# Small runs in four column quarters: output columns instead of chunks

## The chip, the core and the metric

The kernel runs on one core of a Trainium2 chip. A core has TensorE (matrix products; its weight loads are a row of their own in the trace), VectorE (DVE), ScalarE (ACT), GpSimd (POOL) and SyncE (SP, which here only issues DMA transfers). The metric is the device time of one launch in microseconds (us).

## What is computed

Three stages follow each other: a windowed attention, a mixture of experts with one expert per token, and a dense two-layer net. The change lies in the second:

```python
# x: 2304 tokens x 512, eight experts, w1[e]: 512 x 1024, w2[e]: 1024 x 512
e_idx = argmax(x @ w_gate + modality_bias[modality_id])
for e in range(8):
    mask = e_idx == e
    h = maximum(x[mask] @ w1[e], 0)
    out[mask] = gate_w[mask] * (h @ w2[e])
```

All of it is float32.

## The kernel before

Tokens are sorted by expert, and the experts are worked off in **steps** of 256 tokens (a "wide" run). A step has two halves. `half_a` makes the hidden layer in eight blocks of 128 rows (`l1_wide`, `fb` = 0 to 7), `half_b` the output in four blocks (`l2_wide`, `d` = 0 to 3). Operands of the wide run are split into a high and a low part, so that each product is three matmuls (`three`, line 644). Of each block ScalarE writes the high part (line 654 or 663) and VectorE the low part (line 655). Between the blocks other work is woven in by hand: the split of the next expert's weights (`resplit`, line 203, only where the expert changes), the conversion of the dense stage's weights from 64 bits (`cv`, lines 960 to 972, most of VectorE's work here), and the **small run**.

A small run takes what an expert has left over, at most 32 tokens (`SB` = 32), with unsplit float32 weights (`raw`). Whether a step has one is known only on the chip, so each piece stands in a branch (`small`, line 668). Its pieces are spread over the step: `small_x` at block 0 of `half_a`, `small_1` at block 2, `small_h` at block 4, `small_2` at block 0 of `half_b`, `small_y` at 2, `small_out` at 3. In step 1 they come later. Steps 7 and 8 stand in a branch of their own (`either`) with a wide and a narrow arm.

A stationary operand of 32 tokens fills only 32 of TensorE's 128 columns, so the small matmuls are put in the four quarters of 32 columns, whose results land in partitions 0 to 31, 32 to 63 and so on. Before the change each quarter takes another **chunk** of the sum. In `small_1` the quarters hold the four chunks of the 512 inputs, and each streams all 512 columns of a half of w1: two halves, eight matmuls. What stands in the four bands of 32 partitions are four partial sums. ScalarE copies them to `hs`; `small_h` transposes 128 x 128 pieces (four per half, eight in all); and `sum_h` on VectorE adds the bands (two reductions) and clips at zero. `small_2` does the same with the eight chunks of the hidden layer, two per quarter, `small_y` transposes four pieces, and `sum_y` adds their bands. `sum_h` and `sum_y` stand outside the branch: they run in each of the steps 1 to 8, small run or not.

`self.b.A`, `X` and `B` are banks of the accumulator memory (PSUM): `A` and `B` are those of `l1_wide` and `l2_wide`, `X` those of the transposes. In the trace `raw`, `hs`, `ps_e`, `ps_s`, `ps_r` keep their names, `x32` is `x` and `h32` is `h`. The dense stage begins with line 1419, after fourteen filler matmuls (line 865).

Of the kernel before, what the change touches and what calls it, by code (L numbers as in the profile page):

```python
# [10 lines left out]
F32 = mybir.dt.float32  # L11
# [7 lines left out]
ALU = mybir.AluOpType  # L19
AX = mybir.AxisListType  # L20
# [4 lines left out]
HP = H // 2  # L25
# [25 lines left out]
SB = 32  # L51
# [91 lines left out]
class Banks:  # L143
# [12 lines left out]
    def rest(self, st):  # L156
        self.early.close()
        ps = st.enter_context(self.tc.tile_pool(name="ps_e", bufs=1, space=PSUM, reuse_waits="tile"))
        p = [ps.tile([128, 512], F32, name=f"ps_e{i}") for i in range(4)]
        self.A[2:] = p[0:2]  # L160
        self.B = p[2:]
# [44 lines left out]
class Route:  # L206
# [54 lines left out]
    def columns(self, a, b, hi, width, c0=0):  # L261
        V = self.tc.nc.vector
        bc = [128, b - a, width]
        tau = self.cs[:, C_TAU + c0:C_TAU + c0 + width]
        hv = self.hv[:, a:b, 0:width]
        V.tensor_tensor(hv, tau.unsqueeze(1).to_broadcast(bc), hi[:, a:b].unsqueeze(2).to_broadcast(bc), op=ALU.is_equal)
        V.tensor_tensor(hv, hv, self.cs[:, C_VAL + a:C_VAL + b].unsqueeze(2).to_broadcast(bc), op=ALU.mult)

# [17 lines left out]
    def pick(self):  # L286
        nc, oh, n, cum = self.tc.nc, self.oh, N0_T, self.cum
        V = nc.vector
        r = self.before(self.banks.s[1], 0, n)
        V.tensor_tensor(self.v[:, 0:n], r[:, 0:n, :], oh[:, 0:n, :], op=ALU.mult)  # L290
        V.tensor_copy(cum, r[:, n, :])
        yield
# [240 lines left out]
class Moe:  # L533
# [18 lines left out]
    def rest(self, st):  # L552
        one = st.enter_context(self.tc.tile_pool(name="m_two", bufs=1))
        self.hidden(one)
        self.hs = one.tile([128, 2, 512], F32, name="hs")
        self.x32 = one.tile([128, HP, SB], F32, name="x32")
        self.h32 = one.tile([128, 8, SB], F32, name="h32")
        self.xg3 = one.tile([SB, XW], F32, name="xg3")
        self.xg[1] = [one.tile([128, XW], F32, name=f"xgb{i}") for i in range(2)]
# [117 lines left out]

    def small_1(self, s):
        nc, raw = self.tc.nc, self.w.keep
        for h in range(2):  # L680
            for c in range(HP):
                nc.tensor.matmul(self.b.B[h][SB * c:SB * c + SB, :], self.x32[:, c, :], raw[2 * h + c // 2][:, c % 2, :],
                                 start=True, stop=True)
            nc.scalar.copy(self.hs[:, h, :], self.b.B[h])

    def bands(self, ps, n):
        return ps.rearrange("p (f j t) -> p f t j", f=n, t=SB)

    def small_h(self, s):
        nc = self.tc.nc  # L690
        for h in range(2):
            ps = self.b.X[h]
            for f in range(4):
                q = slice(f * 128, (f + 1) * 128)
                nc.tensor.transpose(ps[:, q], self.hs[:, h, q], self.ident)

    def sum_h(self):
        V = self.tc.nc.vector
        for h in range(2):
            V.tensor_reduce(self.h32[:, 4 * h:4 * h + 4, :], self.bands(self.b.X[h], 4), axis=AX.X, op=ALU.add)  # L700
        V.tensor_scalar(self.h32, self.h32, 0.0, None, op0=ALU.max)

    def small_2(self, s):
        nc, raw = self.tc.nc, self.w.keep
        for f in range(8):
            j = SB * (f % 4)
            nc.tensor.matmul(self.b.A[0][j:j + SB, :], self.h32[:, f, :], raw[4 + f // 2][:, f % 2, :],
                             start=(f < 4), stop=(f >= 4))
        nc.scalar.copy(self.hs[:, 0, :], self.b.A[0])

    def small_y(self, s):
        nc = self.tc.nc
        ps = self.b.A[1]
        for c in range(HP):
            q = slice(c * 128, (c + 1) * 128)
            nc.tensor.transpose(ps[:, q], self.hs[:, 0, q], self.ident)

    def sum_y(self):
        self.tc.nc.vector.tensor_reduce(self.x32, self.bands(self.b.A[1], HP), axis=AX.X, op=ALU.add)

    def small_out(self, s):
        self.tc.nc.scalar.copy(self.xy[:, :, bass.ds(self.regs[s]["so"], SB)], self.x32)

    def close_gap(self):
        tc, nc, xy = self.tc, self.tc.nc, self.xy
# [53 lines left out]
    def half_a(self, s, wide, work, rt=None):  # L779
        at = {7: self.small_x} if s == 1 else {0: self.small_x, 2: self.small_1, 4: self.small_h}  # L780
        for fb in range(8):
            if s == 1 and fb == 2:
                self.small_ids(rt, work)
            if s == 1 and fb == 6:
                self.scale(2)
            if s == 1 and fb == 6:
                self.load_regs("sm", R_SM, 1, 5, [ENG.PE, ENG.Activation])
                self.scale3(1)
            if s > 1 and fb in (1, 3, 5):
                self.resplit(s, fb + 1, fb + 3)  # L790
            if fb in at:
                self.small(s, at[fb])
                if at[fb] == self.small_h:
                    self.sum_h()
            if s == 1 and fb == 1:
                self.resplit(1, 4, 8)
            if wide:
                self.l1_wide(fb)
                if s > 1 or fb > 1:
                    next(work, None)  # L800
                    next(work, None)
            if s > 1 and fb == 3:
                self.load_w(s, 0, 4)
        if s == 1:
            self.small(s, self.small_1)
            self.load_w(s, 0, 4)
        for _ in work:
            pass

    def half_b(self, s, wide, work, rt=None):  # L810
        late = s == 1
        off = bass.ds(self.regs[s]["off"], 256)
        for d in range(HP):
            if late and d == 1:
                self.load_regs("sm", R_SM, 5, 10, [ENG.PE, ENG.Activation])
                self.small(s, self.small_h)
                self.sum_h()
                rt.positions()
            if d == (3 if late else 0):
                self.small(s, self.small_2)  # L820
                self.load_w(s, 4, 8)
            if wide and s != 8 and d == (2 if late else 0):
                self.tx(s + 1, 0)
                self.tx(s + 1, 1)
            if not late and d == 2:
                self.small(s, self.small_y)
                if s > 0:
                    self.sum_y()
            if not late and d == 3:
                self.small(s, self.small_out)  # L830
            if wide:
                self.l2_wide(d, off)
            if d < 3:
                for _ in range(6):
                    next(work, None)
            if d == 2:
                self.scale3(s + 1)
                self.resplit(s + 1, 0, 2)
        if late:
            self.small(s, self.small_y)  # L840
            self.sum_y()
            self.small(s, self.small_out)
        for _ in work:
            pass
# [783 lines left out]
```

## Time and profile before

| | us |
|---|---|
| median of three runs | 771.34 (769.26 to 773.08) |
| the profiled execution | 769.39 |
| its span, first to last instruction | 767.6 |
| TensorE busy | 739.3 (96%) |
| TensorE weight loads busy | 658.5 (86%) |
| VectorE busy | 491.3 (64%) |
| ScalarE busy | 387.4 (50%) |
| five small runs, start of `small_1` | 177.0, 206.7, 236.4, 266.1, 322.2 |

Busy time of TensorE overlaps with itself: a matmul's bar is longer than the distance to the next one's start, so here distances between starts are read, not bars. Times in a timeline count from the span's start; "x16" is the number of instructions in a merged row, and the second column is its length from the first start to the last end.

### The profile page before, as it was taken

Reading aid. Unit: us, or ns where it says so; the run is one execution under the profiler, and the core shown is the slowest. Engines: PE = TensorE matmul, PEld = TensorE weight load, DVE = VectorE, ACT = ScalarE, POOL = GpSimd, SP = SyncE. Lnnn points to the kernel's source line nnn. Section 1 sums busy time; section 2 is a strip of 40 time slices with the busy share of each in tenths; the row PEclk is TensorE's granted clock in tenths of the full one; section 3 lists DMA queues with packets and bytes.
Section 4 is the critical chain, followed back from the end, with each engine's and each line's share of the span. In section 5 each row is a group of like instructions: output and inputs, shape, how many; then the busy total and the mean of one; then the engine's idle time right before and its main releaser. Section 6 shows DMA issues by size and latency. Waiting matters only on the chain. (4 is left out here: it accounts for less than half of the span.)

```text
span 767.6 us, 15236 instructions
## 1 busy us (share of the span) xinstructions
PE 739.3 (96%) x5537; PEld 658.5 (86%) x5539; DVE 491.3 (64%) x1149; ACT 387.4 (50%) x1008; POOL 99.3 (13%) x99
## 2 busy tenths in 40 slices
PE   8999879999999999999799999999999999999996
PEld 4888669988998899889799889888889888988895
DVE  3678886773887878986487777864444464344341
ACT  4878753223323323442376666775445566454453
POOL 3325542230110100000000000011000003000003
PEclk9999999999999999999999999999999999999999
DMA  7789951269898967932257777488544556455512
GB/s 205 201 234 296 268 174 44 59 186 331 292 324 275 336 193 253 318 115 75 80 183 286 275 266 284 164 298 304 192 151 163 219 219 227 159 198 216 190 55 82
DMA packets 66189, 161.05 MB, mean 210 GB/s; under 512 B 8416, under 2 KB 25824, under 8 KB 60080
## 3 DMA queue, kind: packets, MB, share of 16 engines
q1 hardware_dynamic: 62592, 148.58, 57.0%
q0 software_dynamic: 3360, 11.01, 4.3%
q8 instruction: 49, 0.80, 0.4%
q14 instruction: 44, 0.36, 0.1%
q10 hardware_dynamic: 144, 0.29, 0.1%
HBM read 118.82 MB, written 41.04 MB: 208 GB/s over the span
## 5 line engine op out<-in xcount | busy, mean ns | idle before, releaser
L1439 DVE SCALAR_TENSOR_TENSOR t<-x,t 128x384 f32<-128x384 f32 x92 | 51.4, 558 | 80.0 <-ACT t L1432 79.8
L1462 PE MATMUL d_o<-d_ob,gh 128*128 128x512 f32 x288 | 89.6, 392 | 0.0
L1462 PE MATMUL d_o<-d_plain,gh 128*128 128x512 f32 x288 | 89.6, 392 | 0.0
L644 PE MATMUL ps_e<-hh,whi 128*128 128x256 f32 x288 | 82.9, 288 | 2.0 <-PEq L668 0.9
L644 PE MATMUL ps_e<-hl,whi 128*128 128x256 f32 x288 | 81.1, 282 | 0.0
L644 PE MATMUL ps_e<-hh,wlo 128*128 128x256 f32 x288 | 81.1, 281 | 0.0
L1431 ACT ACTIVATE t<-x 128x384 f32<-128x384 f32 x92 | 48.3, 525 | 52.5 <-DVE x L1452 52.5
L1447 DVE TENSOR_TENSOR gl<-t,gh 128x384 fp32r<-128x384 f32 x96 | 53.2, 554 | 17.8 <-ACT gh L1440 15.7
L1440 ACT CAST gh<-t 128x384 fp32r<-128x384 f32 x96 | 49.4, 514 | 29.6 <-DVE t L1439 29.3
L1452 DVE TENSOR_TENSOR x<-d_y,d_u 128x384 f32<-128x384 f32 x46 | 25.5, 554 | 53.1 <-ACT d_u L1543 53.1
L1462 PEld LDWEIGHTS d_o<-d_plain,gh 128*128 128x128 f32 x288 | 52.9, 188 | 6.1
L1462 PEld LDWEIGHTS d_o<-d_ob,gh 128*128 128x128 f32 x288 | 52.8, 188 | 5.7
L644 PEld LDWEIGHTS ps_e<-hh,whi 128*128 128x128 f32 x288 | 54.5, 189 | 3.1 <-issue 2.3
L1462 PE MATMUL d_o<-d_ob,gl 128*128 128x512 f32 x144 | 57.2, 397 | 0.0
L1462 PE MATMUL d_o<-d_plain,gl 128*128 128x512 f32 x144 | 57.1, 396 | 0.0
L1543 ACT COPY d_u<-d_x 128x384 f32<-128x384 f32 x46 | 22.0, 479 | 65.1 <-PE d_x L1419 65.1
L644 PEld LDWEIGHTS ps_e<-hh,wlo 128*128 128x128 f32 x288 | 54.5, 189 | 0.0
L644 PEld LDWEIGHTS ps_e<-hl,whi 128*128 128x128 f32 x288 | 54.4, 189 | 0.0
L663 ACT COPY xy<-ps_e 128x256 f32 (+1 forms) x36 | 13.4, 373 | 79.6 <-PE ps_e L644 65.1
L1432 ACT ACTIVATE t<-t 128x384 f32<-128x384 f32 x96 | 50.5, 526 | 3.0
L1471 POOL DMA_INDIRECT out<-o,pid x18 | 17.9, 995 | 248.4 <-ACT o L1470 246.6
L1200 ACT ACTIVATE p<-ps_s,nb 128x96 f32<-128x96 f32 x144 | 47.1, 341 | 2.7 <-issue 0.4
(441 smaller groups left out, 1922.8 us busy)
## 6 DMA issues: line engine op xcount, KB each, us to landing
raw<-in_w SPq DMA_DIRECT2D x48, 512.0 KB, 7.1
d_ab<-cache SPq DMA_DIRECT2D x15, 1024.0 KB, 6.2
d_ab<-cache SPq DMA_DIRECT2D x15, 768.0 KB, 4.3
r<-in_w_in SPq DMA_DIRECT2D x16, 512.0 KB, 5.8
r<-in_w_out SPq DMA_DIRECT2D x16, 512.0 KB, 5.4
wsc<-cva SPq DMA_DIRECT2D x32, 256.0 KB, 4.2
cache<-d_ab SPq DMA_DIRECT2D x8, 1024.0 KB, 5.0
d_ob<-cache SPq DMA_DIRECT2D x8, 1024.0 KB, 7.5
```

Of the source, the lines that this page charges most:

```text
L644: self.tc.nc.tensor.matmul(ps, a, b, start=(i == 0 and j == 0), stop=(i == n - 1 and j == 2))
L663: nc.scalar.copy(self.xy[:, d, off], ps)
L1200: nc.scalar.activation(p[:, j, :], s[:, j, :], ACTF.Exp, scale=scale, bias=nb[:, j:j + 1], accum_out=su[:, j:j + 1])
L1431: nc.scalar.activation(b.t, x, ACTF.Relu, scale=0.5, bias=0.5)
L1432: nc.scalar.activation(b.t, b.t, ACTF.Square)
L1439: nc.vector.scalar_tensor_tensor(b.t, x, 1.0, b.t, op0=ALU.max, op1=ALU.min)
L1440: nc.scalar.copy(b.h, b.t)
L1447: nc.vector.tensor_tensor(b.l, b.t, b.h.bitcast(F32), op=sub)
L1452: nc.vector.tensor_tensor(x, bank, other, op=add)
L1462: nc.tensor.matmul(po[i], a[:, q], o[:, x, f, :], start=(first and j == 0), stop=(last and j == 2))
L1471: nc.gpsimd.indirect_dma_start(out=outs[n][:, :], out_offset=bass.IndirectOffsetOnAxis(ap=pid[:, n:n + 1], axis=0), in_=t, in_offset=None)
L1543: nc.scalar.copy(part[("p1", "u2", "u3")[j // 2]], bank)
```

## The change

Each quarter now makes **its own output columns** over all chunks. In `small_1` quarter `j` streams columns 256 j to 256 j + 255 of the hidden layer (of w1's half `j // 2`) for chunk 0, 1, 2, 3 in turn and sums them in its band of one bank: 16 matmuls of 256 columns in place of 8 of 512. `hs` is then 128 x 256 instead of 128 x 1024, `small_h` needs two transposes instead of eight, and what comes out is already summed: `relu_h` clips it in one VectorE instruction. `small_2` gives each quarter 128 of the 512 output columns over all eight chunks: 32 matmuls of 128 columns in place of 8 of 512. `small_y` needs one transpose instead of four, `sum_y` falls away, and `small_out` copies from the bank.

```diff
     def small_1(self, s):
         nc, raw = self.tc.nc, self.w.keep
-        for h in range(2):
-            for c in range(HP):
-                nc.tensor.matmul(self.b.B[h][SB * c:SB * c + SB, :], self.x32[:, c, :], raw[2 * h + c // 2][:, c % 2, :],
-                                 start=True, stop=True)
-            nc.scalar.copy(self.hs[:, h, :], self.b.B[h])
+        ps = self.b.B[0][:, 0:256]
+        for c in range(HP):
+            for j in range(4):
+                q = slice(j % 2 * 256, j % 2 * 256 + 256)
+                nc.tensor.matmul(ps[SB * j:SB * j + SB, :], self.x32[:, c, :], raw[2 * (j // 2) + c // 2][:, c % 2, q],
+                                 start=(c == 0), stop=(c == HP - 1))
+        nc.scalar.copy(self.hs, ps)
...
     def small_h(self, s):
-        nc = self.tc.nc
-        for h in range(2):
-            ps = self.b.X[h]
-            for f in range(4):
-                q = slice(f * 128, (f + 1) * 128)
-                nc.tensor.transpose(ps[:, q], self.hs[:, h, q], self.ident)
-
-    def sum_h(self):
-        V = self.tc.nc.vector
-        for h in range(2):
-            V.tensor_reduce(self.h32[:, 4 * h:4 * h + 4, :], self.bands(self.b.X[h], 4), axis=AX.X, op=ALU.add)
-        V.tensor_scalar(self.h32, self.h32, 0.0, None, op0=ALU.max)
+        for k in range(2):
+            q = slice(k * 128, (k + 1) * 128)
+            self.tc.nc.tensor.transpose(self.b.X[0][:, q], self.hs[:, q], self.ident)
+
+    def relu_h(self):
+        self.tc.nc.vector.tensor_scalar(
+            self.h32.rearrange("p (j k) t -> p k j t", k=2),
+            self.b.X[0][:, 0:256].rearrange("p (k j t) -> p k j t", k=2, t=SB), 0.0, None, op0=ALU.max)
 
     def small_2(self, s):
         nc, raw = self.tc.nc, self.w.keep
+        ps = self.b.A[0][:, 0:128]
         for f in range(8):
-            j = SB * (f % 4)
-            nc.tensor.matmul(self.b.A[0][j:j + SB, :], self.h32[:, f, :], raw[4 + f // 2][:, f % 2, :],
-                             start=(f < 4), stop=(f >= 4))
-        nc.scalar.copy(self.hs[:, 0, :], self.b.A[0])
+            for j in range(4):
+                nc.tensor.matmul(ps[SB * j:SB * j + SB, :], self.h32[:, f, :], raw[4 + f // 2][:, f % 2, j * 128:(j + 1) * 128],
+                                 start=(f == 0), stop=(f == 7))
+        nc.scalar.copy(self.hs[:, 0:128], ps)
 
     def small_y(self, s):
-        nc = self.tc.nc
-        ps = self.b.A[1]
-        for c in range(HP):
-            q = slice(c * 128, (c + 1) * 128)
-            nc.tensor.transpose(ps[:, q], self.hs[:, 0, q], self.ident)
-
-    def sum_y(self):
-        self.tc.nc.vector.tensor_reduce(self.x32, self.bands(self.b.A[1], HP), axis=AX.X, op=ALU.add)
+        self.tc.nc.tensor.transpose(self.b.A[1][:, 0:128], self.hs[:, 0:128], self.ident)
 
     def small_out(self, s):
-        self.tc.nc.scalar.copy(self.xy[:, :, bass.ds(self.regs[s]["so"], SB)], self.x32)
+        self.tc.nc.scalar.copy(self.xy[:, :, bass.ds(self.regs[s]["so"], SB)],
+                               self.b.A[1][:, 0:HP * SB].rearrange("p (c t) -> p c t", c=HP))
```

At the places that called `sum_h` stands `relu_h`; the calls of `sum_y` are gone.

TensorE around `small_2` of step 2 (the difference; `xgb` is the gathered input of the next step, whose eight transposes follow): one row of eight 512-column matmuls gives way to one of 32 with 128 columns, at the same place.

```order
 L668 COMPARE_AND_BRANCH
-L707 MATMUL ps_s_81<-raw,h_2059 32x512 x8
-L668 UNCONDITIONAL_BRANCH x2
-L775 UNCONDITIONAL_BRANCH
+L703 MATMUL ps_s_81<-raw,h_2059 32x128 x32
+L668 UNCONDITIONAL_BRANCH x2
+L765 UNCONDITIONAL_BRANCH
 L635 MATMUL ps_r<-cs,xgb_2061 128x128 x4
 L635 MATMUL ps_s_83<-cs,xgb_2062 128x128 x4
```

The quarters follow each other within a chunk, so that neighbours in this row lie in different quarters, as before.

VectorE in step 3, around `sum_h` before the change (`cva` and `r` are the conversion, `hl` is a low part of the hidden layer):

```order
L655 SCALAR_TENSOR_TENSOR hl_118<-ps_e_2038,hh_117 128x256
L964 TENSOR_SCALAR r_3202<-r_3202 128x512
L700 TENSOR_REDUCE h_2059<-ps_r 128x128
L775 UNCONDITIONAL_BRANCH
L700 TENSOR_REDUCE h_2059<-ps_s_83 128x128
L701 TENSOR_SCALAR h_2059<-h_2059 128x256
L655 SCALAR_TENSOR_TENSOR hl_2056<-ps_s_81,hh_2055 128x256
```

and the same place after it:

```order
L655 SCALAR_TENSOR_TENSOR hl_118<-ps_e_2038,hh_117 128x256
L951 TENSOR_SCALAR r_3240<-r_3240 128x512
L694 TENSOR_SCALAR h_2059<-ps_r 128x2x4x32
L765 UNCONDITIONAL_BRANCH
L655 SCALAR_TENSOR_TENSOR hl_2056<-ps_s_81,hh_2055 128x256
```

Three instructions have become one; their neighbours stand as they did.

## Rows read from the trace of the kernel before

**Rows 1.** Busy time by stretch: stretch, length, PE, PEld, DVE, ACT, POOL, clock, DMA.

```profile
173.00:293.00 120.00, 119.78 (x1014) 106.46 (x1015) 88.03 (x189) 36.92 (x86) 10.29 (x11) 1.00 0.86 291
293.00:374.00 81.00, 78.26 (x637) 73.41 (x636) 61.87 (x121) 29.35 (x59) 4.89 (x5) 1.00 0.51 170
374.00:381.40 7.40, 3.66 (x18) 2.74 (x17) 3.58 (x8) 3.12 (x8) 0.00 (x0) 1.00 0.20 63
```

**Rows 2.** One line's instructions, `small_1` (ns min/median/max; first and last start).

```profile
L682 PE MATMUL ps_e<-raw,x x80: 592/592/618, 177.0 to 323.5; 128*32 128x512 f32 x80
```

**Rows 3.** Timeline of TensorE and its weight loads in the first small run.

```profile
177.03 0.16 PEld L682 LDWEIGHTS ps_e<-raw,x 128*32 128x32 f32 x8
177.03 1.92 PE L682 MATMUL ps_e<-raw,x 128*32 128x512 f32 x16
177.49 0.13 PEld L682 LDWEIGHTS ps_e<-raw,x 128*32 128x32 f32 x4 [0.30 <-issue]
177.91 0.13 PEld L682 LDWEIGHTS ps_e<-raw,x 128*32 128x32 f32 x4 [0.30 <-issue]
178.88 0.39 PE L644 MATMUL ps_e<-xh,whi 128*128 128x256 f32 x1
...
181.85 0.60 PE L695 MATMUL ps_r<-cs,hs 128*128 128x128 f32 x4
182.29 0.60 PE L695 MATMUL ps_s<-cs,hs 128*128 128x128 f32 x4
182.65 0.36 PE L644 MATMUL ps_s<-xh,whi 128*128 128x256 f32 x1
...
188.35 0.28 PE L644 MATMUL ps_e<-xl,whi 128*128 128x256 f32 x1
188.56 1.92 PE L707 MATMUL ps_s<-raw,h 128*32 128x512 f32 x16
```

**Rows 4.** Attention's matmuls in two column halves: weight loads (timeline, then the line).

```profile
43.29 0.66 PEld L1232 LDWEIGHTS ps_o<-pt,v 96*64 96x64 f32 x20
...
L1232 PEld LDWEIGHTS ps_o<-pt,v x576: 132/138/231, 20.5 to 119.9; 96*64 96x64 f32 x192
```

**Rows 5.** Groups by line: VectorE's sums (busy us, mean ns, idle time before them).

```profile
L719 DVE TENSOR_REDUCE x<-ps_s 128x128 f32<-128x512 f32 x8 | 5.5, 685 | 1.6 <-PEq L668 1.6
L700 DVE TENSOR_REDUCE h<-ps_r 128x128 f32<-128x512 f32 x8 | 5.5, 685 | 1.8 <-PEq L668 1.8
L701 DVE TENSOR_SCALAR h<-h 128x256 f32<-128x256 f32 x8 | 2.4, 294 | 0.3
```

**Rows 6.** Timeline before `small_2` of step 7: VectorE, ScalarE, then TensorE.

```profile
329.73 0.68 DVE L700 TENSOR_REDUCE h<-ps_r 128x128 f32<-128x512 f32 x1
...
331.59 2.35 DVE L203 TENSOR_TENSOR wlo<-raw,whi 128x1024 fp32r<-128x1024 f32 x2
333.86 0.42 DVE L655 SCALAR_TENSOR_TENSOR hl<-ps_s,hh 128x256 fp32r<-128x256 f32 x1
...
329.79 1.98 ACT L201 CAST whi<-raw 128x1024 fp32r<-128x1024 f32 x2
...
333.51 0.28 PE L644 MATMUL ps_e<-xl,whi 128*128 128x256 f32 x1
334.38 2.04 PE L707 MATMUL ps_s<-raw,h 128*32 128x512 f32 x16 [0.59 <-PE ps_e L644]
```

**Rows 7.** Timeline from the last expert step to the dense stage.

```profile
374.45 0.68 DVE L719 TENSOR_REDUCE x<-ps_s 128x128 f32<-128x512 f32 x1
...
374.30 3.37 PE L865 MATMUL ps_r<-whi 128*128 128x512 f32 x14
381.44 0.58 PE L1419 MATMUL d_x<-d_B110h,d_plain 128*128 128x384 f32 x2 [3.77 <-DMA d_wo<-wsc]
```

**Rows 8.** Timeline of TensorE where step 8 jumps over a small run's piece.

```profile
362.00 0.28 PE L644 MATMUL ps_e<-xl,whi 128*128 128x256 f32 x1
362.43 0.35 PE L644 MATMUL ps_e<-hh,whi 128*128 128x256 f32 x1
```

More of the change, by code (lines that the diff above doesn't have):

```diff
@@ L554, in rest @@
         self.hidden(one)
-        self.hs = one.tile([128, 2, 512], F32, name="hs")
+        self.hs = one.tile([128, 256], F32, name="hs")
         self.x32 = one.tile([128, HP, SB], F32, name="x32")
@@ L679, in small_1 @@
         nc, raw = self.tc.nc, self.w.keep
-        for h in range(2):
-            for c in range(HP):
-                nc.tensor.matmul(self.b.B[h][SB * c:SB * c + SB, :], self.x32[:, c, :], raw[2 * h + c // 2][:, c % 2, :],
-                                 start=True, stop=True)
-            nc.scalar.copy(self.hs[:, h, :], self.b.B[h])
-    def bands(self, ps, n):
-        return ps.rearrange("p (f j t) -> p f t j", f=n, t=SB)
-    def small_h(self, s):
-        nc = self.tc.nc
-        for h in range(2):
-            ps = self.b.X[h]
-            for f in range(4):
-                q = slice(f * 128, (f + 1) * 128)
-                nc.tensor.transpose(ps[:, q], self.hs[:, h, q], self.ident)
@@ L793, in half_a @@
                 if at[fb] == self.small_h:
-                    self.sum_h()
+                    self.relu_h()
             if s == 1 and fb == 1:
@@ L816, in half_b @@
                 self.small(s, self.small_h)
-                self.sum_h()
+                self.relu_h()
                 rt.positions()
@@ L826, in half_b @@
                 self.small(s, self.small_y)
-                if s > 0:
-                    self.sum_y()
             if not late and d == 3:
@@ L840, in half_b @@
             self.small(s, self.small_y)
-            self.sum_y()
             self.small(s, self.small_out)
```

## The prediction

> **What bounds the kernel now.** I read the busy time by stretch first, since the share over the whole span mixes three stages. From 173 to 293 us, where four of the five small runs stand, TensorE is busy 119.78 of 120 us, VectorE 88 and ScalarE 37 [rows 1]. To 374 us, with the fifth small run and two narrower steps, it is 78.26 of 81. Only the passage to the dense stage has a hole (3.66 of 7.40). So in the expert stage TensorE sets the pace, and what is taken from or added to its stream moves the stage's end one for one. What VectorE or ScalarE saves is worth nothing unless a TensorE wait on it shows.
>
> Next, the first small run in the timeline. The bars can't be summed: a `small_1` pass shows 592 ns [rows 2], yet sixteen fit into 1.92 us [rows 3]. I read starts instead. The eighty passes are five runs of sixteen, and a run has eight matmuls, so each float32 matmul is two passes. The later weight loads come in fours at 177.49 and 177.91, 0.42 us apart, and (1.92 − 0.59) / 3 = 0.44 gives the same: four passes, one for each column quarter, go on together, and a **round** of four takes 0.43 us for 512 columns. Quarters do overlap before the change; it must keep that.
>
> **Term 1, transposes.** Eight become two and four become one: nine fewer per run. Four take 182.29 − 181.85 = 0.44 us from start to start [rows 3], so one takes 0.11. TensorE stands behind them without a gap. 9 × 0.109 = 0.98 us less per run.
>
> **Term 2, matmul passes.** The work in columns stays, the pieces get smaller. `small_1`: 16 matmuls of two passes are 32 passes, or 8 rounds of 256 columns, in place of 4 rounds of 512. `small_2`: 64 passes, or 16 rounds of 128, in place of 4 of 512. No row has such rounds of quarters. The rows on both sides are the 512-column rounds (0.43 us) and attention's matmuls in two halves, 64 columns wide, which are ten rounds in 0.66 us: (0.66 − 0.14) / 9 = 0.058 us each [rows 4]. A line through both gives 0.111 us for 128 columns and 0.217 for 256. `small_2`: 16 × 0.111 = 1.78 for 4 × 0.43 = 1.72, +0.06. `small_1`: 8 × 0.217 = 1.74, +0.02. I take +0.08 per run. Bounds: 0, if time goes by columns alone; and a floor for each pass, since a half's pass took 0.058 / 2 = 0.029 us whatever set that. Four such are 0.116, so `small_2` takes 16 × 0.116 = 1.86 (+0.14) and a run +0.16. Below nothing I see no reason: no column is left out.
>
> Terms 1 and 2 are −0.90 per run (−0.98 to −0.82), for five runs **−4.5 us** (−4.9 to −4.1).
>
> **Term 3, VectorE and ScalarE.** Per step VectorE loses two sums of 685 ns and a clip of 294, which become one clip that reads the accumulator bank; and `sum_y`, 685 [rows 5]. The new clip lies between 0.29, the clip now, and 0.42, a low part of equally many columns that reads a bank too [rows 6]. So some 2 us leave each step, and ScalarE's copies into `hs` shrink from three of 512 columns to one of 256 and one of 128. Through 293 us TensorE never waits for either, and this buys nothing. One place differs: step 7. There `small_2` starts 334.38 − 333.51 = 0.87 us after the last `l1_wide` matmul [rows 6], against 188.56 − 188.35 = 0.21 in the first run [rows 3]: 0.66 us idle. The row names its own engine, but what had just ended is VectorE's low part (333.86 + 0.42 = 334.28). That was queued behind the weight split, and this behind the sums. The order of these neighbours is unchanged. Sums and clip there cost 0.68 + 0.68 + 0.29 = 1.65 us, the new clip at most 0.42, so VectorE comes 1.2 us earlier; but the split also needs ScalarE's high part, which ends at 329.79 + 1.98 = 331.77, just after the split's start, so the first of the two pieces may not move and only the second can. I take −0.55, between 0 (ScalarE holds it all) and −0.66 (all idle time goes; then the last matmul is itself what comes last).
>
> **Term 4, the way to the dense stage.** Line 1419 starts 3.77 us after the fillers, put down to a DMA of `d_wo` [rows 7]. The fillers follow TensorE's last step, and the transfer is issued behind VectorE's last work, which follows TensorE too. So I let the whole passage slide with the stage: 0. `sum_y` at 374.45 disappears; if the passage hangs on it, up to another 0.6 us goes.
>
> **Other things that move.** The first two `raw` tiles are read until the end of `small_1` in either order, so their refill comes no earlier than now; DMA is 0.86 busy there [rows 1], but TensorE waits for none. `small_out` now reads the bank and not `x32`: one semaphore of TensorE instead of one of VectorE, later than `small_y` by a whole block, and behind it on ScalarE stands only the next high part. All this I cost at nothing; the cover is that ScalarE is busy 37 of 120 us.
>
> **Sum.** −4.5 − 0.55 = −5.05 us, between −4.1 and −6.2 (−4.9 − 0.66 − 0.6). The profiled execution took 769.39 us (span 767.6 and 1.8 around it), so it would take 764.3. It lies 1.95 below the median of the runs shown, 771.34; from the median the time is **766.3 us**. The bounds give 765.1 to 767.2.
>
> **Rivals.**
>
> *Weight loads come into the open: slower.* There are twice the loads in `small_1` and four times in `small_2`, 24 rounds in place of 8. A quarter's weights have 0.11 us of cover in `small_2` where they had 0.43. If a round's loads had to wait until the round before is done, each round would be longer by about 0.11 us, the distance between a load of four and the next at the rate of four in 0.13 [rows 3]: 24 × 0.11 = 2.64 per run, less 0.98, +1.66, five times +8.3, or 779.6 us. It decides from 0.98 / 24 = 0.04 us per round. Against it: the halves load in 132 to 138 ns and yet follow each other at 58 ns a pair [rows 4], and the eight loads at 177.03 stand within 0.16 us while the first passes run [rows 3]. For it: no row has quarters with so few columns. 0.05. [...]
>
> *The longer branch bodies cost a fetch: slower.* The body of `small_2` becomes four times as long (64 passes with their loads for 16), and steps without a small run jump over it. A jump over the short body takes 362.43 − 362.00 = 0.43 us from matmul to matmul [rows 8]. If the longer jump leaves what the engine has fetched, the nearest price is the idle time at the end of the stage, where TensorE also branches away: 3.77 [rows 7], 3.34 more. Skips in steps 1, 6 and 8 and the arms not taken in 7 and 8 make five places: 5 × 3.34 − 5.05 = +11.7, or 783.0 us. It decides from 5.05 / 5 = 1.0 us a place. Against it: three of the five steps with such places lie between 293 and 374 us, where TensorE idles 2.74 us in all [rows 1], so that no jump costs nearly that today. 0.04. [...]
>
> *The dense stage does not move: no change.* If line 1419's start hangs on transfers with their own schedule, TensorE ends 5 us earlier and waits 5 us longer: 771.3 us. For it: the row blames a DMA [rows 7], and the DMA share is 0.51 in the stretch before it. Against: the transfer is issued only after VectorE's last work, and the share is 0.20 there [rows 1]. 0.08.
>
> **How the numbers follow.** Forecast 0.83, the three rivals 0.05, 0.04 and 0.08. About 0.5%, 3.9 us, is what a measurement of this kernel can tell from no change: the three runs span 3.8. The forecast's −4.1 to −6.2 lies just beyond, and the scatter of the medians puts some 0.12 of its 0.83 within: faster 0.71, same 0.12 + 0.08 = 0.20, slower 0.09. For the range I take the bounds, 765.1 and 767.2, and add the distance between profile and median (2.0) on both sides, then widen above to 770 for a forecast that reaches the dense stage only in part: 763 to 770.
>
> **What would show it.** In the profile after: 32 passes of 256 columns and 64 of 128 columns per run, five runs; from `small_1`'s start to the next `l1_wide` matmul still about 1.85 us, `small_2` 1.7 to 1.9; a line of ten transposes and one of five; steps of about 28.8 us where two small runs stood 29.7 apart; `relu_h` at 0.29 to 0.42 us; `small_2` of step 7 some 0.2 us behind line 644; line 1419 near 376.4. The prediction falls if the weight loads of `small_2` have gaps of passes between them (first rival), if line 644 waits behind a skipped body for longer than now (second), or if line 1419 stays at 381 (third).

## The result, and the profile after

The changed kernel takes 761.92 us (median of four runs, 760.82 to 762.92), the kernel before, beside it, 771.51 (769.26 to 773.08). The ratio is 0.988, 95% interval 0.9861 to 0.9898: 9.6 us faster, where 5.05 were forecast and 763 was the range's lower end. The profiled execution took 762.92 us (span 761.1), so this profile lies 1.0 above its median, and the one of before 2.1 below its own. The two profiles therefore differ by 6.47 only.

Both executions can be laid on each other matmul by matmul, since nothing but the small runs' lines differs. Read from starts:

| stretch | before | after | difference |
|---|---|---|---|
| to the first `small_1` (attention, routing, steps 0 and 1) | 177.03 | 178.81 | +1.78 |
| from there to the last `l1_wide`/`l2_wide` matmul (line 644) | 197.14 | 191.82 | −5.32 |
| from there to the first dense matmul (line 1419, now 1406) | 7.26 | 4.98 | −2.28 |
| from there to the start of the last matmul | 379.32 | 378.59 | −0.73 |
| behind it and around the span | 8.63 | 8.72 | +0.09 |

The first row is not the change's: no changed matmul has run by then, and in the profiles of the experiments below, which leave that part alone too, the first `small_1` starts anywhere from 177.0 to 181.0 us. The rest makes −8.2. What lacks to 9.6 lies within the scatter of either kernel's four runs. Of 18 later executions of the kernel before, the ten with a mean granted clock of 0.987 or less took 770.5 to 773.2 us and the four with 0.993 to 0.995 took 767.8 to 769.6, and its profiled one, at 0.993, is of the second sort.

The forecast was made for the second row. Its rows in the changed kernel, first run (timeline: start, length, then line and shape; PE is TensorE):

```profile
178.81 1.93 PE L684 MATMUL ps_e<-raw,x 128*32 128x256 f32 x32
180.67 0.39 PE L644 MATMUL ps_e<-xh,whi 128*128 128x256 f32 x1
...
183.53 0.28 PE L644 MATMUL ps_e<-xl,whi 128*128 128x256 f32 x1
183.65 0.38 PE L691 MATMUL ps_r<-cs,hs 128*128 128x128 f32 x2
183.79 0.36 PE L644 MATMUL ps_s<-xh,whi 128*128 128x256 f32 x1
...
189.72 1.95 PE L703 MATMUL ps_s<-raw,h 128*32 128x128 f32 x64
191.60 0.66 PE L635 MATMUL ps_r<-cs,xgb 128*128 128x128 f32 x4
...
198.24 0.27 PE L708 MATMUL ps_s<-cs,hs 128*128 128x128 f32 x1
198.27 0.36 PE L644 MATMUL ps_e<-hh,whi 128*128 128x256 f32 x1
```

Against [rows 3]: `small_1` holds TensorE for 180.67 − 178.81 = 1.86 us (178.88 − 177.03 = 1.85 before), `small_2` for 1.88. The transposes of `small_h` take 183.79 − 183.65 = 0.14, where 182.65 − 181.85 = 0.80 stood; `small_y`'s one takes 0.03. Per run that is −0.98 by transposes and +0.04 by passes.

The third row of the table is the one that the forecast put at nothing. Timeline after, from the last matmul of the stage:

```profile
370.75 3.37 PE L852 MATMUL ps_r<-whi 128*128 128x512 f32 x14
375.62 0.58 PE L1406 MATMUL d_x<-d_B110h,d_plain 128*128 128x384 f32 x2 [1.49 <-DVE d_B110h L1387]
376.24 0.44 PE L1406 MATMUL d_x<-d_B110l,d_plain 128*128 128x384 f32 x1
```

The idle time ahead of the dense stage is 1.49 us, and ends with VectorE's cast of the operand; in [rows 7] it was 3.77 and put down to a DMA. VectorE was not late there: before the change the same cast ended at 378.85 + 0.36 = 379.21, 2.2 us ahead of the matmul.

```profile
378.85 0.36 DVE L1400 CAST d_B110h<-xy 128x384 fp32r<-128x384 f32 x1 [3.71 <-DVEq L139]
```

What TensorE did in that idle time stands in the instructions of line 139, where the jump over all steps from 9 on ends (count, then shortest/median/longest ns, then first and last start; PEldq is TensorE's sequencer). Before, then after:

```profile
L139 PEldq EVENT_SEMAPHORE  x2: 51/51/51, 377.7 to 380.7; - x2
...
L139 PEldq COMPARE_BRANCH  x1: 3668/3668/3668, 373.9 to 373.9; - x1
```

```profile
L139 PEldq EVENT_SEMAPHORE  x2: 51/51/51, 374.2 to 374.3; - x2
...
L139 PEldq COMPARE_BRANCH  x1: 3674/3674/3674, 370.4 to 370.4; - x1
```

The jump takes 3.67 us in both, while the fillers still run. Behind it stand two semaphore instructions of 51 ns each, neither of which waits. After the change they follow each other by 0.15 us; before, 3.03 us lay between them, in which TensorE executed nothing. A transfer of 16 KB of instructions started at 378.36 and ended at 379.50 in that time, which suggests that the engine was out of code; the experiments test it. This pause held the dense stage.

Behind it the clock was lower, too. Windows of the first dense matmuls (stretch, length, busy times, then the granted clock, DMA share, GB/s), before and then after:

```profile
381.44:384.80 3.36, 3.36 (x12) 3.36 (x13) 2.66 (x6) 0.20 (x1) 0.00 (x0) 0.60 0.94 253
```

```profile
375.62:378.50 2.88, 2.84 (x15) 2.53 (x16) 2.88 (x7) 2.88 (x8) 0.00 (x0) 1.00 0.66 156
```

After 3.77 us idle the granted clock was 0.60 in this window: 0.50 from 382.20 to 385.50 us, where the matmuls of 384 columns start 0.32 us apart, and, behind the window, 1.00 from 385.60 to 389.00, where they start 0.17 us apart. After 1.49 us idle it was 1.00. Over the first 4 us of the dense stage this brings 1.2 us more, of which 0.5 is given back some 20 us later, where a matmul of the changed kernel waits for `d_T40l` of VectorE: hence −0.73 in the table's fourth row. This price is not the pause's alone: in two experiments below (the first half alone, and 64 columns) the dense part was 1.0 us longer than the changed kernel's without a pause, after 1.64 and 1.59 us idle. With the first half alone the granted clock here was 0.68; with 64 columns that of the whole execution was 0.987, against 0.992 in the changed kernel's.

### The profile page after: what moved, and what is told of

Same layout as the page of the kernel before. It is cut to its first block, busy times and chain, and to the rows that moved or that the text cites. A ratio compares the mean times of both kernels' runs of the same rounds, so it can differ in the third digit from the quotient of the medians.

```text
span 761.1 us, 15743 instructions
## 1 busy us (share of the span) xinstructions
PE 735.3 (97%) x5814; PEld 662.6 (87%) x5814; DVE 477.2 (63%) x1125; ACT 381.7 (50%) x1003; POOL 99.2 (13%) x99
## 4 chain that ended last, share of the span: by engine, by line
PE 31%; issue 15%; DMA 1%; DVE 1%; POOL 1%; ACT 1%; POOLq 0%; SPq 0%; ACTq 0%
PE d_o L1449 16%; PE d_x L1406 8%; PE d_y L1406 6%; POOL out L1458 1%; DMA cache<-d_ob 1%; DMA d_wo<-wsc 1%; DVE d_rT L1381 0%; DVE d_ob L1075 0%; DVE gl L1434 0%; POOLq L1611 0%; SPq L1012 0%; ACT d_ob L1073 0%; ACT o L1457 0%; DVE x L1439 0%; ACT t L1418 0%
```

## The experiments

**Is it the place of TensorE's code?** To the kernel before, matmuls are added that are never executed, in a step that is jumped over:

```diff
+        if s == 10:
+            for _ in range(40):
+                tc.nc.tensor.matmul(self.b.X[0], self.w.hi[0][:, 0, 0:128], self.w.hi[0][:, 1, :], start=True, stop=True)
```

> The kernel before, with 40 filler matmuls (80 instructions of TensorE) put into step 10, which is jumped over with all steps from 9 on, so that nothing more is executed and only TensorE's code behind them stands at other places. Theory (where TensorE's jump to the dense stage lands in its code sets a second wait): the pause between the two semaphore instructions of line 139 at 377.7 and 380.7 us goes, line 1419 starts 2.3 us earlier after the last line 644 (7.2 us becomes about 4.9), its first thirty matmuls no longer take 0.32 us but 0.17, and the time falls by about 3.7 us, to some 767.8. Rival (the change's own work brought the passage forward, by the sum taken off VectorE or by the DMA of d_wo): nothing moves, 771.5.

Measured: 766.35 us against 771.03, ratio 0.9955 (0.9936 to 0.9975). The stage is as long as ever (197.16 us), the passage is 4.93 in place of 7.26, and the rest of TensorE's stream 378.09 in place of 379.32.

```profile
374.83 3.37 PE L865 MATMUL ps_r<-whi 128*128 128x512 f32 x14
379.64 0.58 PE L1422 MATMUL d_x<-d_B110h,d_plain 128*128 128x384 f32 x2 [1.45 <-DVE d_B110h L1403]
```

With `sum_y` and everything else of the old kernel in place, code that nobody runs makes it faster: by 4.7 us between the medians, by 3.5 (1.9 to 4.9) from the ratio. VectorE's chain and the DMA are as they were, and so are out as causes.

**Can the pause be brought back?** The same lines in the changed kernel, first 85 of them. These are 170 instructions, which by a rough count of the author's put the jump's target near where it was before the change. The count took it that places in the code repeat every 256 instructions, an assumption which no run had shown.

> The changed kernel with 85 fillers in step 10, also never executed. [...] Theory of the landing place: the second pause comes back, line 1406 starts about 2 to 3 us later after the last line 644 (4.99 becomes 7 to 8), the first dense matmuls are slow again, and the time rises by 3 to 4 us, to about 765.5. Rival (the shorter VectorE chain): nothing moves, 761.9.

Measured: 762.29 us, passage 4.92: the pause of 3 us did not come, and the time is the changed kernel's. The rough count was off. Counted in the compiled programs, TensorE's code behind the jump is moved by 2023 instructions against the kernel before, 25 short of a multiple of 256. If the pause belongs to a place that comes once in 256 instructions, as assumed, TensorE should stop not after one instruction but after 26. Behind the jump come seven semaphore instructions, ten weight loads and nine matmuls, 26 in all, and then the tenth matmul is late: it starts 0.42 us behind the ninth, in the changed kernel 0.17 (rows here, then there). Its operand had been ready since 376.41.

```profile
377.09 0.33 PE L1409 MATMUL d_x<-d_B210l,d_plain 128*128 128x384 f32 x1
377.51 0.51 PE L1409 MATMUL d_x<-d_B211h,d_plain 128*128 128x384 f32 x2
```

```profile
377.40 0.33 PE L1406 MATMUL d_x<-d_B210l,d_plain 128*128 128x384 f32 x1
377.57 0.51 PE L1406 MATMUL d_x<-d_B211h,d_plain 128*128 128x384 f32 x2
```

With 97 matmuls the code is moved, by the count, by one instruction less than a multiple of 256:

> The changed kernel with 97 fillers in step 10 (never executed) in place of 85. Counted in the compiled program, TensorE has 16498 instructions before the change (114 above a multiple of 256), 18351 after it (175), 18521 with 85 fillers (89), 18026 with the second half alone (106), and 18545 here (113); the dense stage behind the landing place is the same in all. The kernel before ran one instruction behind line 139's jump and then stood; the second half alone, 8 lower, ran nine. Theory of the landing place: here two instructions run and then the pause of 2 to 3 us comes, line 1406's equal starts 7.2 to 7.5 us after the last line 644 in place of 4.98, the first thirty or so dense passes are at the lower clock, and the time is 3 to 4 us above the changed kernel's, 765 to 766. Rival (the changed kernel no longer has what caused the pause): 762.

Measured: 766.06 us against 770.89 for the kernel before (0.993, 0.9913 to 0.9947). The passage is 7.16 us, the stage 191.81, unchanged.

```profile
370.82 3.37 PE L852 MATMUL ps_r<-whi 128*128 128x512 f32 x14
377.86 0.98 PE L1409 MATMUL d_x<-d_B110h,d_plain 128*128 128x384 f32 x2 [3.67 <-DMA d_wo<-wsc]
```

The window behind it, with the granted clock third from the end:

```profile
377.86:381.20 3.34, 3.34 (x11) 3.34 (x12) 2.63 (x6) 0.59 (x2) 0.00 (x0) 0.50 0.89 260
```

Both semaphore instructions of line 139 run (374.23 and 374.38), then nothing until 377.31: two instructions, as the count had it, and the profile blames `d_wo` once more. The clock is 0.50 behind it, and at the end this trace is 3.9 us behind the changed kernel's. With the pause in both, the change is worth 4.8 us (770.89 − 766.06); without it in either, 4.4 (766.35 − 761.92, from two sessions; 5.1 between their means). Both are near the 5.05 of the forecast.

**The two halves of the change, each alone.** In the first, `small_1`, `small_h` and `relu_h` are the new ones, in the second `small_2`, `small_y` and `small_out`, without `sum_y`.

```diff
...
-                    self.sum_h()
+                    self.relu_h()
...
```

> The kernel before with only small_1, small_h and relu_h changed; small_2, small_y and sum_y stay. Theory (TensorE's stream carries the gain one for one): per small run 0.65 us less by the six transposes and nothing from the passes, five times 3.2, and all of step 7's 0.63 us, since only the sums of h stand ahead of its weight split: 3.9 us from the first small run to the last line 644. Rival (step 7 gained because small_2 changed): 3.2. The passage to the dense stage is free to go either way, since the code behind moves by 17 x 20 = 340 instructions.

```diff
...
-                if s > 0:
-                    self.sum_y()
...
```

> The kernel before with only small_2, small_y and small_out changed, and sum_y gone. Theory: per small run 0.33 us less by three transposes and 0.03 more by the passes, five times 0.30 = 1.5 us from the first small run to the last line 644, and step 7 keeps its wait ahead of small_2. If the gain of the passage came from sum_y, which stands as VectorE's last work before the jump, the passage is shorter here and not in the run that changes the first half; if it is the landing place (code moved by 17 x 90 = 1530, 250 more than five times 256, so 6 short of the old place), the passage stays long here.

Measured: the first half takes 764.54 us (0.992, 0.989 to 0.995) with a stage of 193.46, so −3.68; the second 768.13 (0.9965, 0.9951 to 0.998) with 195.58, so −1.56. Together −5.24 of the −5.32. Step 7 goes with the first half: there `small_2` starts 0.32 us after the matmul ahead of it, with the second half alone 0.87 as in [rows 6]. The first half's passage is 5.13 us, without the pause, and yet the granted clock fell behind it (0.68, third from the end) and the dense part takes 379.62 us:

```profile
376.43:379.80 3.37, 3.33 (x12) 3.02 (x13) 3.36 (x8) 2.33 (x6) 0.00 (x0) 0.68 0.77 226
```

On the passage the second expectation was half wrong: it did get shorter, to 4.68 us, but the pause had only moved to a place behind the first dense matmul:

```profile
373.98 3.37 PE L857 MATMUL ps_r<-whi 128*128 128x512 f32 x14
378.54 0.41 PE L1411 MATMUL d_x<-d_B110h,d_plain 128*128 128x384 f32 x1 [1.19 <-DVE d_B110h L1392]
380.80 0.44 PE L1411 MATMUL d_x<-d_B110h,d_plain 128*128 128x384 f32 x1 [1.85 <-issue]
```

"issue" is the profile's word for a wait for nothing that it shows. This program's code is moved by 8 instructions less than a multiple of 256, and the pause came after nine instructions where it had come after one. With the runs above, four kernels stop where the count puts it, relative to each other: after 1, 2, 9 and 26 instructions, for 3.03, 2.93, 2.26 and 0.24 us. The four fit one place in the code, a **border**, behind which the instructions come late: 3.0 to 3.6 us after the first semaphore instruction of line 139 in all four. Read so, what stands between target and border runs in that time, and what is left of it is the pause. The moves were 8 × 256 − 1, 6 × 256 − 8 and 8 × 256 − 25 instructions, which fits the assumed 256 between borders; 128 or 512 would fit these runs as well. Here too the clock fell (0.61 from 380.80 to 384.20 us), and the dense part is the longest of all (381.44 us).

**What brought step 7 its gain?** Two reductions go back on VectorE there, with no use of their results:

```diff
+                    if s == 7:
+                        for _ in range(2):
+                            self.tc.nc.vector.tensor_reduce(
+                                self.x32, self.b.X[0].rearrange("p (f j t) -> p f t j", f=HP, t=SB), axis=AX.X, op=ALU.add)
                     self.relu_h()
```

> The changed kernel with two reductions of 128 x 512 on VectorE put back ahead of relu_h in step 7 alone; their results are not used. Theory (step 7 gained its 0.63 us because VectorE's queue ahead of the weight split got 1.2 us shorter): the split and the low part come later by about 1.3 us again, less what ScalarE hides, and small_2 starts some 0.6 to 0.85 us later after the last line 644 of half_a, 0.85 in place of 0.21; the rest of the stage is unchanged. Rival (the wait went because small_2 or its semaphores changed): it starts 0.21 us after line 644 still.

Measured: 762.12 us in one run, with a stage 1.32 us longer (193.14) behind a first part that happened to be 1.44 shorter. The wait is back, and larger than forecast: `small_2` starts 1.64 us after line 644, not 0.85.

```profile
330.66 0.41 DVE L655 SCALAR_TENSOR_TENSOR hl<-ps_s,hh 128x256 fp32r<-128x256 f32 x1
...
329.54 0.28 PE L644 MATMUL ps_e<-xl,whi 128*128 128x256 f32 x1
331.18 0.49 PE L703 MATMUL ps_s<-raw,h 128*32 128x128 f32 x9 [1.36 <-issue]
```

In all three kernels `small_2` starts 0.1 us after the end of VectorE's second low part: 334.28 and 334.38 before, 331.21 and 331.30 after, 331.07 and 331.18 here. So VectorE's queue sets this start. TensorE comes to it earlier here than before, since `small_h` is 0.65 us shorter, and VectorE's new clip is 0.12 us longer than the old (418 ns for 294): together the 0.77 by which the wait is longer. The expectation forgot both.

**Must the quarters alternate?** The loops of the small matmuls are turned round, so that neighbours use the same quarter:

```diff
-        for c in range(HP):
-            for j in range(4):
+        for j in range(4):
+            for c in range(HP):
...
-        for f in range(8):
-            for j in range(4):
+        for j in range(4):
+            for f in range(8):
```

> The changed kernel with the loops of small_1 and small_2 turned round: quarter outside, chunk inside, so that neighbours in TensorE's stream lie in the same quarter; the same matmuls and results. Theory (four passes of different quarters go on together only while they stand next to each other): small_1 takes 32 x 0.213 = 6.8 us and small_2 64 x 0.107 = 6.8 in place of 1.87 each, about 9.9 us per run, 50 us in all, some 811. Rival (the engine runs quarters side by side in whatever order they come, or the time of a pass is set by its issue): 1.9 us each, 762.

Measured: 793.79 us in one run.

```profile
177.04 4.59 PE L684 MATMUL ps_e<-raw,x 128*32 128x256 f32 x32
181.57 0.39 PE L644 MATMUL ps_e<-xh,whi 128*128 128x256 f32 x1
...
190.61 5.96 PE L703 MATMUL ps_s<-raw,h 128*32 128x128 f32 x64
196.50 0.33 PE L635 MATMUL ps_r<-cs,xgb 128*128 128x128 f32 x1
```

`small_1` holds TensorE for 4.52 us and `small_2` for 5.89, in place of 1.86 and 1.88; 6.67 more per run, 33 in five. The direction is the theory's, the size is not: a pass of 256 columns behind another of its quarter takes 4.52 / 32 = 0.141 us and not 0.213, one of 128 takes 0.092 and not 0.107.

**How small may the pieces get?** `small_2` in pieces of 64 columns:

```diff
+        for i in range(2):
             for f in range(8):
                 for j in range(4):
-                nc.tensor.matmul(ps[SB * j:SB * j + SB, :], self.h32[:, f, :], raw[4 + f // 2][:, f % 2, j * 128:(j + 1) * 128],
+                    k = j * 128 + i * 64
+                    nc.tensor.matmul(ps[SB * j:SB * j + SB, i * 64:i * 64 + 64], self.h32[:, f, :], raw[4 + f // 2][:, f % 2, k:k + 64],
```

> The changed kernel with small_2 in pieces of 64 columns: 64 matmuls, 128 passes, in place of 32 and 64; first the left half of every quarter's columns over all chunks, then the right half. Theory A (time goes by columns: 128 passes in 32 rounds at half of 0.107): small_2 still takes about 1.9 us. Theory B (a pass has a floor of 29 ns, as the attention's halves and small_2's 1.885 / 64 both show): 128 x 0.029 = 3.8 us, 1.9 more per run, 9.5 in all, about 771.

Measured: 771.5 us in one run, as theory B has it, and yet theory B is wrong. The 128 passes take 1.93 us, 0.015 each: no floor of 0.029.

```profile
191.92 1.99 PE L705 MATMUL ps_s<-raw,h 128*32 128x64 f32 x128
193.85 0.32 PE L635 MATMUL ps_r<-cs,xgb 128*128 128x128 f32 x1
```

That the total fits is chance. Of the 9.6 us above the changed kernel 2.2 lie ahead of the first small run, 1.0 in the dense stage, and 5.4 in the stage. Most of these 5.4 went into waits of the wide run's matmuls; three of them have no releaser, of which neither kernel shows one from 176 to 370 us (line waited for: us in total, times, longest; then one of them in the timeline):

```profile
PE ps_e L644 <- issue: 3.7, 3, 2.0
```

```profile
225.73 0.28 PE L644 MATMUL ps_e<-hh,whi 128*128 128x256 f32 x1
227.98 0.39 PE L644 MATMUL ps_e<-hh,wlo 128*128 128x256 f32 x1 [1.97 <-issue]
```

Here too TensorE starts nothing between 225.73 and 227.98, and a transfer of 16 KB of instructions runs from 225.76 to 226.71. The pause ends 1.27 us behind it, the other two 1.32 and 1.22 behind such a transfer; before the change, 380.74 − 379.50 = 1.24. It looks like the same pause, come perhaps by twice as many instructions per `small_2`. That such a pause moves with the place of the code was shown at the dense stage only; that TensorE waits for code here is the author's reading of the trace.

## Why the prediction was wrong

**Term 1, transposes, was right to the hundredth**: −0.65 and −0.33 per run, 0.98. **Term 2, passes, was right in kind**: +0.04 per run, where +0.08 was taken and 0 to +0.16 allowed. That is halfway between time by columns alone (0) and the line between the column counts (+0.08); the floor of 0.029 us per pass, the upper bound, does not exist for quarters (0.015). Both steps stand, and the stage moved one for one with TensorE, as [rows 1] had it: five runs gave 4.7 us, forecast 4.5.

**Term 3 was right**: the gap ahead of `small_2` in step 7 fell from 0.87 to 0.32 us, the 0.55 that was taken; `small_2` itself also lost the slow start it had there (1.97 to 1.89). The new clip takes 418 ns, at its bound. The stage in all: −5.32, forecast −5.05.

**Term 4 failed.** "I let the whole passage slide with the stage: 0", with at most 0.6 us more, rested on the label of [rows 7], a DMA of `d_wo`, which line 1419 doesn't read. Ahead of the matmul lay a pause of 3.03 us on TensorE, which went when nothing but the place of the code was changed (7.26 us of passage became 4.93); by the count, the jump's target stood one instruction ahead of a border in the code. The change makes TensorE's code 1853 instructions longer (counted in the compiled programs) and so moves that target; the pause went, 2.28 us of it on the path, and in this profile the lower clock behind it (0.60, after the change 1.00), 0.73 at the end. Why the code behind a border comes that late, and how far apart borders are, no run shows. `sum_y`, the 0.6 in the bound, had no part that shows: with it and without the pause the passage is 4.93 us.

**The rivals.** The weight loads stayed covered (line, then ns min/median/max):

```profile
L703 PEld LDWEIGHTS ps_s<-raw,h x320: 106/110/110, 189.7 to 332.9; 128*32 128x32 f32 x160
```

The passes of 128 columns follow each other at 1.885 / 64 = 0.029 us, though each has a load of 110 ns and all use the same 128 rows. In the run with the loops turned round, where neighbours share the quarter too, it is 0.092; whether that is a load in the open was not separated. The third rival, no movement, fell with [rows 7]'s label. The second, a wait for code, fits what was found, with the wrong sign. It priced a code fetch at 3.34 us from the idle time in [rows 7], and thereby had the pause in hand, but counted only new ones that longer bodies could bring, not the old one that they could take away. At these jumps the traces do show waits, though not what for: TensorE's at line 139 takes 3.67 us, and in the kernel before the next instructions of ScalarE and VectorE come 2.7 and 3.0 us behind theirs. The cost that surprised was a second one, at a border behind the target.

## What to carry to other kernels

Here an idle time of 3.77 us was put down to a transfer that the matmul behind it doesn't read. Before a price of zero is built on such a label, look at what the engine's own instructions do in the idle time: here 3.03 us of it lay between two instructions that don't wait, and this pause moved with edits that only changed the length of the code ahead of it. And a change that moves code should be measured at two places of the code, with some instructions that are never run, lest such a pause be booked to it: here it was about 4 of the 9.6 us (3.5 to 4.7 in the kernel before, 4.1 in the changed one, 3.9 between two traces of it).

## What was not expected of the hardware

- A jump's target one, two, nine or 26 instructions ahead of a border in the code (places by the count) came with a second pause, of 3.0, 2.9, 2.3 and 0.24 us; in the changed kernel and in the old one with 80 instructions more there was none.
- Passes that follow each other in one quarter take 0.141 us (256 columns) and 0.092 us (128); four quarters in turn take 0.058 and 0.029 per pass. So four side by side are 2.4 and 3.1 times as fast as one after another, not four times.
- Quarter passes of 64 columns follow each other at 0.015 us, half the 0.029 of the attention's halves of the same width [rows 4].
